# Attention with top-k and an ELU feed-forward on one core: one score burst over four PSUM banks, and a gate summed in SBUF

## The chip, the core and the metric

The kernel runs on one core of a Trainium2 chip. A core has TensorE (PE, with its weight loads shown as PEld), VectorE (DVE), ScalarE (ACT), GpSimd (POOL) and the DMA queue of SyncE (SP). The engines run their own instruction streams and wait for each other by semaphores. The metric is the time on the device in microseconds (us). PSUM, into which TensorE writes, has eight banks of 512 fp32 columns in each of 128 partitions, as the kernel's tiles use it.

## What is computed

For 8 batches of 8 heads with 576 positions of 64 features, each query keeps the 32 largest of its 576 scores; softmax over these, then the product with v. The 4608 rows of 512 features go through a feed-forward block with ELU.

```python
scores = scale * np.matmul(q, k.transpose(0, 1, 3, 2))
kth = np.partition(scores, -top_k, axis=-1)[..., -top_k:-top_k + 1]
mask = scores >= kth
scores = np.where(mask, scores, -1000000000.0)
scores = scores - np.max(scores, axis=-1, keepdims=True)
attn = np.exp(scores)
attn = attn / (np.sum(attn, axis=-1, keepdims=True) + 1e-09)
x = np.matmul(attn, v)          # heads side by side: (4608, 512)
h = x @ w_in                    # 512 -> 2048
g = np.where(h > 0.0, h, np.exp(np.minimum(h, 0.0)) - 1.0)
out = g @ w_out                 # 2048 -> 512
```

## The kernel before

The work is cut into 144 steps. A step is one tile of 128 queries for a pair of heads (`Step`). A batch has 576 = 4 x 128 + 64 query rows, so 16 normal steps and two remainder steps, in which four heads share a tile of 64-row halves (`u.heads`). Steps are ordered by batch; pairs of tiles with one pair of heads form a `Group`, which is closed (product with v) once.

A step passes through five stages, each in a later turn of the loop at L617: scores are made two steps ahead (`scores`, L280), the selection of the 32 largest runs in the current step (`select`, L322), the mask and the exponential one step later (`mask`, L345), the scaling by the reciprocal at that step's end (`normalise`, L362), the transposes of the 9 chunks of 128 score columns two steps later (`turn`, L375), and after the last tile of a group the product with v (`attend`, L397). The selection is done by VectorE alone: per row of scores four MAX8 (each finds eight maxima) and three MATCH_REPLACE8 (which take them out), for two heads.

`scores` works by halves. For each half of 288 key columns two matmuls (one a head, each in two fp32 passes) write two banks of the tile `ps`, and one ScalarE activation copies both out with the scale (L297). The pool `ps_sc` has one such tile, so the second half waits for the first's copy. Head 0 of a pair uses rows 0 to 63 of TensorE's array and head 1 rows 64 to 127: the profile prints such a matmul as 64*128 (rows by columns of the array used), a hidden matmul as 128*128 and one of `attend` as 128*64. In `attend` the chunks 0 to 3 use all 128 key rows, and the last chunk, which holds the 64 remaining keys of both heads, uses 64 rows each: 64*64.

`transpose_qk` (L236) turns k and q of a pair of heads, four transposes each, then the remaining 64 rows of both with three small transposes (64*128), which go out with one copy (L262).

The feed-forward work is cut into pieces in `ffn_pieces` (L457) and handed out by `feed` (L577), four times a step. `hidden(f)` computes 128 of the 2048 hidden features of a block of one to three tiles (L471), and ScalarE makes n = exp(-relu(-h)) with two activations (L479, L480). The gate is max(n - 1, h), one VectorE instruction with h from PSUM (L451). `close_gates` issues these late, at the next `feed`, at the next project piece, or when two are open. `project` multiplies the gates with w_out into a PSUM bank over four pieces (L489) and ScalarE copies the result out (L498). How much is handed out follows from costs (`HIDDEN`, `PROJECT`) and the step by which each block's work is due.

PSUM is used up: `ps_sc` has two banks, `ps_t` (transposes and `attend`) three, `ps_f` (hidden and project) three. From step 8 on (`tight`) the order of TensorE, ScalarE, VectorE and GpSimd is that of the program text (`manual_schedule`, L644); before, a scheduler orders it. During the first eight steps the weights, which arrive as 64-bit floats, are decoded to fp32 in pieces (`decode_piece`).

Of the kernel before, what the change touches and what calls it, by code (L numbers as in the profile page):

```python
# [9 lines left out]
ALU = mybir.AluOpType  # L10
# [70 lines left out]
def kernel(  # L81
# [35 lines left out]
    etpool = pool("et", 2)  # L117
    small = pool("small", 4)
    xtpool = pool("xt", 2)
    fpool = pool("f", 2)  # L120
    opool = pool("o", 1)
    ps_sc = pool("ps_sc", 1, space=PSUM)
    ps_t = pool("ps_t", 3, space=PSUM)
    ps_f = pool("ps_f", 3, space=PSUM)
    late = {}
    raws = ExitStack()
    early = raws.enter_context(tc.tile_pool(name="early", bufs=1))
    rawpool = raws.enter_context(tc.tile_pool(name="raw", bufs=3))

    ident = const.tile([P, P], FP32, tag="ident", name="ident")  # L130
# [59 lines left out]
    def hook():  # L190

        if not decode:
            return
        decode.pop(0)()
        if not decode:
            raws.close()
            late["g"] = ctx.enter_context(tc.tile_pool(name="g", bufs=2))
            late["x"] = ctx.enter_context(tc.tile_pool(name="x", bufs=2))

# [9 lines left out]
    loaded, kqT, vT = {}, {}, {}  # L209

    def load_qk(b, hp):
        for name, src in (("k", k), ("q", q)):
            t = ldpool.tile([P, J + 1, 2, D], FP32, tag=name + "in", name=name + "in")
            for hh in range(2):
                nc.sync.dma_start(
                    t[:, 0:J, hh, :],
                    src[b, 2 * hp + hh, 0:JP, :].rearrange("(p j) d -> p j d", j=J),
                )
            nc.sync.dma_start(
                t[0:R, J, :, :],  # L220
                src[b, 2 * hp : 2 * hp + 2, JP:S, :].rearrange("h p d -> p h d"),
            )
            loaded[b, hp, name] = t

    def load_v(b, hp):
        t = kvpool.tile([P, 2 * J + 1, D], FP32, tag="vT", name="vT")
        for hh in range(2):
            h = 2 * hp + hh
            nc.sync.dma_start(
                t[:, hh * J : (hh + 1) * J, :],  # L230
                v[b, h, 0:JP, :].rearrange("(p j) d -> p j d", j=J),
            )
            nc.sync.dma_start(t[hh * R : (hh + 1) * R, 2 * J, :], v[b, h, JP:S, :])
        vT[b, hp] = t

    def transpose_qk(b, hp):  # L236

        d = kvpool.tile([P, 4 * J + 3, D], FP32, tag="kqT", name="kqT")
        kqT[b, hp] = d[:].rearrange("p c d -> p (c d)")
        srcs = [loaded.pop((b, hp, name)) for name in ("k", "q")]
        for i, src in enumerate(srcs):
            ps = ps_t.tile([P, JP], FP32, tag="t", name="qkps")
            for c in range(J):
                nc.tensor.transpose(  # L247
                    ps[:, c * P : (c + 1) * P],
                    src[:, c, :, :].rearrange("p h d -> p (h d)"),
                    ident[:],  # L250
                )
            c0 = KEYS + i * (2 * J + 1) * D
            nc.scalar.copy(kqT[b, hp][:, c0 : c0 + JP], ps[:])
            yield
        ps = ps_t.tile([P, JP], FP32, tag="t", name="qkps")
        for i, src in enumerate((srcs[0], *srcs)):
            nc.tensor.transpose(  # L257
                ps[:, i * R : (i + 1) * R],
                src[0:R, J, :, :].rearrange("p h d -> p (h d)"),
                ident[0:R, 0:R],  # L260
            )
        nc.scalar.copy(  # L262
            d[:, 0 : 4 * J + 3 : 2 * J + 1, :],
            ps[:, 0 : 3 * R].rearrange("p (a s) -> p a s", a=3),
        )
        yield

    def start_qk(b, hp):
        turning.append(transpose_qk(b, hp))
# [7 lines left out]

    turning = []

    def scores(u, half):  # L280

        if half == 0:
            u.sc = scpool.tile([P, 2, S], FP32, tag="sc", name="sc")
        ps = ps_sc.tile([P, 2, JP], FP32, tag="s", name="scps")
        q0 = QUERIES + u.t.qt * P
        for h, i, rows in u.heads:
            kq = kqT[u.t.b, h // 2]
            part = slice(i * D, (i + 1) * D)
            k0 = (KEYS if i == 0 else 0) + half * HS
            nc.tensor.matmul(  # L290
                ps[rows, i, 0:HS],
                kq[part, q0 : q0 + u.t.ql],
                kq[part, k0 : k0 + HS],
                start=True,
                stop=True,
            )
        nc.scalar.activation(  # L297
            u.sc[:, :, half * HS : (half + 1) * HS], ps[:, :, 0:HS], AF.Copy, scale=scale
        )

    def select_row(u, i):
        if i == 0:
# [72 lines left out]
    def turn(u, chunks):  # L375

        if u.turned:
            return
        g = u.group
        if g.et is None:  # L380
            g.et = etpool.tile([P, 2 * J + 1, len(g.tiles), P], FP32, tag="et", name="et")
        ps = ps_t.tile([P, JP], FP32, tag="t", name="eps")
        sc = u.sc[:, :, :].rearrange("p i s -> p (i s)")
        n = chunks.stop - chunks.start
        for c in range(n):
            c0 = (chunks.start + c) * P
            nc.tensor.transpose(ps[:, c * P : (c + 1) * P], sc[:, c0 : c0 + P], ident[:])  # L387
        nc.scalar.copy(  # L388
            g.et[:, chunks, u.at, :],
            ps[:, 0 : n * P].rearrange("p (c q) -> p c q", c=n),  # L390
        )
        if chunks.stop == 2 * J + 1:
            u.turned = True
            if u.at == len(g.tiles) - 1:
                closing.append(g)

    def attend(g):  # L397
# [3 lines left out]
        for k in range(2 if t.rem else 1):  # L401
            hp = 2 * g.hp + k if t.rem else g.hp
            vt = vT[t.b, hp]
            for c in range(J + 1):
                for i in range(2):
                    rows = slice(0, P) if c < J else slice(i * R, (i + 1) * R)
                    chunk = J if c == J else i * (J + 1) + c
                    w = g.et[rows, chunk, :, :].rearrange("p a q -> p (a q)")
                    cols = slice(0, n)
                    if t.rem:  # L410
                        c0 = R * (k if i == 0 else 1 - k)
                        w = w[:, c0 : c0 + R]
                        cols = slice(k * R, (k + 1) * R)
                    nc.tensor.matmul(  # L414
                        ps[i * D : (i + 1) * D, cols],
                        vt[rows, 2 * J if c == J else i * J + c, :],
                        w,
                        start=(c == 0),
                        stop=(c == J),
                    )  # L420
# [23 lines left out]
            ffn.extend(ffn_pieces(blk))  # L444

    gates = []

    def close_gates():
        for dst, n, ps in gates:
            w = dst.shape[-1]  # L450
            nc.vector.scalar_tensor_tensor(  # L451
                out=dst, in0=n[:, 0:w], scalar=-1.0, in1=ps[:, 0:w],
                op0=ALU.add, op1=ALU.max,
            )
        gates.clear()

    def ffn_pieces(blk):  # L457
        n_tok = blk.slots * P

        def hidden(f):  # L460
# [3 lines left out]
            elif f % NG == 0 and blk.number > 0:  # L464
                g = late["g"].tile([P, NG, T], FP32, tag="g", name="gT")
                blk.gT.append(g[:])
            if len(gates) > 1:
                close_gates()
            ps = ps_f.tile([P, dm], FP32, tag="f", name="hps")
            for i in range(NC):  # L470
                nc.tensor.matmul(  # L471
# [3 lines left out]
                    start=(i == 0),  # L475
                    stop=(i == NC - 1),
                )
            n = fpool.tile([P, T], FP32, tag="n", name="n")
            nc.scalar.activation(n[:, 0:n_tok], ps[:, 0:n_tok], AF.Relu, scale=-1.0)  # L479
            nc.scalar.activation(n[:, 0:n_tok], n[:, 0:n_tok], AF.Exp, scale=-1.0)  # L480
            gates.append((blk.gT[f // NG][:, f % NG, 0:n_tok], n, ps))

        def project(s, part):
            close_gates()
# [91 lines left out]

    def feed(n, share):  # L577

        close_gates()
        fed["at"] = max(fed["at"], n)  # L580
        ahead = [(w - fed["sum"]) / (x - fed["at"]) for x, w in due if x > fed["at"]]
        if ahead:
            fed["over"] += max(0.0, share * min(ahead))
        fed["at"] += share
        while ffn and decoded[0] >= ffn[0][1] and 0.5 * ffn[0][0] <= fed["over"]:
            cost, _, piece = ffn.pop(0)
            fed["over"] -= cost
            fed["sum"] += cost
            piece()
# [5 lines left out]
    load_v(0, 0)  # L595
    start_qk(0, 0)
    turn_qk(True)
    scores(steps[0], 0)
    scores(steps[0], 1)
    load_qk(0, 2)  # L600
    start_qk(0, 1)
    turn_qk(True)
    scores(steps[1], 0)
    scores(steps[1], 1)
    load_qk(0, 3)
    for hp in range(1, NHP):
        load_v(0, hp)
# [9 lines left out]
    for n in range(NS + 3):  # L617
# [2 lines left out]
        ahead, cur, prev, done = step(n + 2), step(n), step(n - 1), step(n - 2)  # L620
        if n < tight:
            turn_qk(True)
            scores(ahead, 0)
            scores(ahead, 1)
            for i in range(2):
                passes = select_row(cur, i)
                next(passes)
# [17 lines left out]
            )  # L645
        passes = select(cur) if cur else iter(range(4))
        if ahead:
            scores(ahead, 0)
        next(passes)
        feed(n, 0.25)  # L650
        if prev:
            mask(prev, 0)
        turn_qk()
        while closing:
            attend(closing.pop(0))
        if ahead:
            scores(ahead, 1)
        next(passes)
        feed(n, 0.25)
        if done:  # L660
# [49 lines left out]
```

## Time and profile before

| | |
|---|---|
| Time, median of 3 runs | 1733.86 us (1732.75 to 1734.05) |
| Profiled execution, its own time | 1732.9 us |
| Span from its first to its last instruction | 1731.0 us |
| Mean granted TensorE clock | 0.975 |
| HBM traffic over the span | 31 GB/s |

The busy share by slice, 43 us each, and the clock that TensorE was granted:

```profile
PE   6468999999999999999999999999999999999999
DVE  6899999999999999999989898999999989997700
PEclk9568999999999999999999999999999999999999
```

The digits are tenths. The first four slices hold the start and the decoding of the weights, with a lower clock; the last two are feed-forward work alone. The largest groups of instructions by line:

```profile
L471 PE MATMUL hps<-xT,w_in 128*128 128x256 f32 (+2 forms) x2432 | 563.7, 378 | 22.8 <-DVE gT L451 15.6
L341 DVE MAX8 m<-wk 128x8 f32<-128x576 f32 x816 | 574.9, 745 | 0.0
L489 PE MATMUL ops<-w_out,gT 128*128 128x512 f32 x1152 | 525.3, 600 | 2.5 <-DVE gT L451 2.5
L290 PE MATMUL scps<-kqT 64*128 64x288 f32 (+1 forms) x1280 | 232.4, 462 | 32.6 <-ACT sc L297 24.3
L371 POOL TENSOR_SCALAR sc<-sc,rec 128x576 f32<-128x576 f32 x288 | 213.9, 752 | 185.1 <-DVE rec L369 175.2
L297 ACT ACTIVATE sc<-scps 128x576 f32<-128x576 f32 x288 | 185.9, 646 | 86.2 <-PE scps L290 81.4
L414 PE MATMUL avps<-et,vT 128*64 128x256 f32 (+5 forms) x2080 | 200.4, 328 | 3.8 <-ACT et L388 3.7
```

A group's line names the source line, engine, operation, output and inputs, the form and the count; behind the bar stand busy time in us, the mean of one in ns, and the engine's idle time just before such instructions with what ended most of it. Matmuls overlap, so the mean of one is longer than its share of TensorE's time; for that one compares start times.

### The profile page before, as it was taken

To read this page: it belongs to the slowest core of one execution; us is meant where nothing else is said; L and a number is where in the kernel's file an instruction comes from. 1 tells how busy PE (TensorE), PEld (TensorE's weight loads), DVE (VectorE), ACT (ScalarE), POOL (GpSimd) and SP (SyncE) were. 2 spreads that over 40 slices of the span, in tenths; PEclk is the share of its full clock that TensorE was granted. 3 is DMA by queue.
4 is the path that set the end of the run, shared out by engine and by line. 5 is a ranking of instruction groups with operands and counts; after the bars stand their busy time and mean duration, and the time that the engine had idled before them with its cause. 6 is when DMAs were issued, how large, how long until landed. Compare 5 with 4: busy or idle time off the path is not lost.

```text
span 1731.0 us, 25867 instructions
## 1 busy us (share of the span) xinstructions
PE 1647.5 (95%) x8592; PEld 1007.8 (58%) x8592; DVE 1544.7 (89%) x3392; ACT 1145.1 (66%) x2509; POOL 407.5 (24%) x1078
## 2 busy tenths in 40 slices
PE   6468999999999999999999999999999999999999
PEld 3245677557474756555456565645547475745565
DVE  6899999999999999999989898999999989997700
ACT  5786787678676867667666675757657585756521
POOL 2674222222222222221212122221222221121100
PEclk9568999999999999999999999999999999999999
DMA  6641021001100110001200111001100000000000
GB/s 155 178 135 44 15 48 34 7 7 42 48 7 7 34 46 23 1 24 31 48 12 1 41 35 34 1 13 42 42 19 1 26 15 27 7 7 7 7 13 12
DMA packets 101125, 56.19 MB, mean 32 GB/s; under 512 B 84096, under 2 KB 92288, under 8 KB 100992
## 3 DMA queue, kind: packets, MB, share of 16 engines
q1 hardware_dynamic: 100992, 54.55, 11.5%
q8 instruction: 67, 1.10, 0.3%
q14 instruction: 66, 0.54, 0.1%
HBM read 45.09 MB, written 9.44 MB: 31 GB/s over the span
## 4 chain that ended last, share of the span: by engine, by line
PE 82%; DVE 8%; ACT 2%; issue 1%; POOL 1%; DMA 0%; ACTq 0%
PE ops L489 28%; PE hps L471 27%; PE avps L414 9%; PE scps L290 9%; PE eps L387 7%; DVE wk L334 3%; DVE m L341 3%; PE qkps L247 1%; DVE m L329 1%; ACT sc L297 1%; DVE gT L451 1%; PE qkps L257 0%; ACT n L480 0%; ACT n L479 0%; DVE wk L311 0%
## 5 line engine op out<-in xcount | busy, mean ns | idle before, releaser
L471 PE MATMUL hps<-xT,w_in 128*128 128x256 f32 (+2 forms) x2432 | 563.7, 378 | 22.8 <-DVE gT L451 15.6
L341 DVE MAX8 m<-wk 128x8 f32<-128x576 f32 x816 | 574.9, 745 | 0.0
L489 PE MATMUL ops<-w_out,gT 128*128 128x512 f32 x1152 | 525.3, 600 | 2.5 <-DVE gT L451 2.5
L471 PEld LDWEIGHTS hps<-xT,w_in 128*128 128x128 f32 x2432 | 406.1, 193 | 143.1 <-DVE gT L451 26.0
L334 DVE MATCH_REPLACE8 wk<-m,wk 128x576 f32<-128x576 f32 x544 | 399.4, 741 | 0.0
L489 PEld LDWEIGHTS ops<-w_out,gT 128*128 128x128 f32 x1152 | 208.7, 190 | 240.4 <-issue 232.5
L367 POOL TENSOR_SCALAR dene<-den 128x2 f32<-128x2 f32 x144 | 33.1, 230 | 1000.2 <-ACT sc L358 999.9
L290 PE MATMUL scps<-kqT 64*128 64x288 f32 (+1 forms) x1280 | 232.4, 462 | 32.6 <-ACT sc L297 24.3
L388 ACT COPY et<-eps 128x512 f32<-128x512 f32 (+1 forms) x432 | 189.8, 474 | 102.4 <-PE eps L387 102.3
L371 POOL TENSOR_SCALAR sc<-sc,rec 128x576 f32<-128x576 f32 x288 | 213.9, 752 | 185.1 <-DVE rec L369 175.2
L357 ACT ACTIVATE sc<-sc,neg 128x576 f32<-128x576 f32 x288 | 224.0, 778 | 48.4 <-POOL neg L354 48.1
L297 ACT ACTIVATE sc<-scps 128x576 f32<-128x576 f32 x288 | 185.9, 646 | 86.2 <-PE scps L290 81.4
L358 ACT ACTIVATE sc<-sc,gap 128x576 f32<-128x576 f32 x288 | 223.1, 775 | 25.3
L479 ACT ACTIVATE n<-hps 128x256 f32<-128x256 f32 (+2 forms) x304 | 111.5, 367 | 144.9 <-PE hps L471 131.9
L387 PEld LDWEIGHTS eps<-ident,sc 128*128 128x128 f32 x1296 | 156.8, 144 | 84.6 <-issue 53.9
L414 PE MATMUL avps<-et,vT 128*64 128x256 f32 (+5 forms) x2080 | 200.4, 328 | 3.8 <-ACT et L388 3.7
L387 PE MATMUL eps<-ident,sc 128*128 128x128 f32 x1296 | 192.1, 282 | 12.3 <-POOL sc L371 11.7
L334 DVE MATCH_REPLACE8 wk<-m,sc 128x576 f32<-128x576 f32 x272 | 199.7, 741 | 0.0
L329 DVE MAX8 m<-sc 128x8 f32<-128x576 f32 x272 | 191.1, 744 | 0.0
L451 DVE SCALAR_TENSOR_TENSOR gT<-n,hps 128x256 f32<-128x256 f32 (+2 forms) x304 | 117.6, 391 | 71.4 <-ACT n L480 70.7
L414 PEld LDWEIGHTS avps<-et,vT 128*64 128x64 f32 (+1 forms) x2080 | 115.4, 138 | 95.0 <-issue 53.8
L290 PEld LDWEIGHTS scps<-kqT 64*128 64x128 f32 (+1 forms) x1280 | 91.5, 180 | 126.0 <-issue 47.9
(40 smaller groups left out, 840.8 us busy)
## 6 DMA issues: line engine op xcount, KB each, us to landing
kin<-in_k_dram SPq DMA_DIRECT2D x64, 128.0 KB, 2.8
qin<-in_q_dram SPq DMA_DIRECT2D x64, 128.0 KB, 2.9
raw<-in_moe_w_in_dram SPq DMA_DIRECT2D x16, 512.0 KB, 4.1
vT<-in_v_dram SPq DMA_DIRECT2D x64, 128.0 KB, 2.3
raw<-in_moe_w_out_dram SPq DMA_DIRECT2D x16, 512.0 KB, 3.3
out_dram<-osb SPq DMA_DIRECT2D x32, 256.0 KB, 2.2
kin<-in_k_dram SPq DMA_DIRECT2D x32, 32.0 KB, 2.5
qin<-in_q_dram SPq DMA_DIRECT2D x32, 32.0 KB, 2.5
```

Source lines behind the costliest of these rows:

```text
L290: nc.tensor.matmul(ps[rows, i, 0:HS], kq[part, q0 : q0 + u.t.ql], kq[part, k0 : k0 + HS], start=True, stop=True,)
L297: nc.scalar.activation(u.sc[:, :, half * HS : (half + 1) * HS], ps[:, :, 0:HS], AF.Copy, scale=scale)
L329: nc.vector.max(found[i], cur[i])
L334: nc.vector.match_replace(wk[i], found[i], cur[i], TAKEN)
L341: nc.vector.max(found[i], cur[i])
L357: nc.scalar.activation(sc, sc, AF.Prelu, bias=neg[:], alpha=STEEP)
L358: nc.scalar.activation(sc, sc, AF.Exp, bias=gap[:], accum_out=u.den[:, i : i + 1])
L371: nc.gpsimd.tensor_scalar(u.sc[:, i, :], u.sc[:, i, :], rec[:, i : i + 1], 1.0, ALU.mult, ALU.mult)
L387: nc.tensor.transpose(ps[:, c * P : (c + 1) * P], sc[:, c0 : c0 + P], ident[:])
L414: nc.tensor.matmul(ps[i * D : (i + 1) * D, cols], vt[rows, 2 * J if c == J else i * J + c, :], w, start=(c == 0), stop=(c == J),)
L471: nc.tensor.matmul(ps[:, 0:n_tok], w_in[:, i, f * P : (f + 1) * P], blk.xT[:, i, 0:n_tok], start=(i == 0), stop=(i == NC - 1),)
L489: nc.tensor.matmul(blk.o[:], blk.gT[f // NG][:, f % NG, s * P : (s + 1) * P], w_out[:, f, :], start=(f == 0), stop=(f == NF - 1),)
```

## The change

Five things are changed together.

1. `scores` makes both halves in one burst. One tile `wide` of four banks, made once, takes the place of `ps_sc`'s tile; each head has two banks, and ScalarE copies one head (2 x 288 columns) at a time. `ps_t` and `ps_f` go from three banks to two. In the loop from step 8 the burst stands at the step's start, followed by `attend`, which stood behind the first feed.
2. Small outputs go to the unused columns of `wide`: the transposes of the remaining k and q rows to bank 1, the single chunk of `turn` to bank 3.
3. The remaining q rows are loaded beside the remaining k rows in one tile, and two full transposes take the place of three small ones. They now come first in `transpose_qk`.
4. In v the remaining rows of the two heads get a slot each, with zeros in the other head's rows (GpSimd memsets), so that `attend` uses all 128 rows in its last chunk too.
5. The gate becomes relu(h) + (n - 1): ScalarE writes relu(h) into the gate with a third activation, and VectorE adds n - 1 there, with both inputs in SBUF. The sums are issued two feeds later, or when four are open; n gets more buffers (`earlyf` 4, `f` 5).

```diff
+    wide = ps_sc.tile([P, 4, JP], FP32, tag="s", name="scps")
-    ps_t = pool("ps_t", 3, space=PSUM)
-    ps_f = pool("ps_f", 3, space=PSUM)
+    ps_t = pool("ps_t", 2, space=PSUM)
+    ps_f = pool("ps_f", 2, space=PSUM)
...
     def load_v(b, hp):
-        t = kvpool.tile([P, 2 * J + 1, D], FP32, tag="vT", name="vT")
+        t = kvpool.tile([P, 2 * J + 2, D], FP32, tag="vT", name="vT")
...
-            nc.sync.dma_start(t[hh * R : (hh + 1) * R, 2 * J, :], v[b, h, JP:S, :])
+            mine = slice(hh * R, (hh + 1) * R)
+            other = slice((1 - hh) * R, (2 - hh) * R)
+            nc.gpsimd.memset(t[other, 2 * J + hh, :], 0.0)
+            nc.sync.dma_start(t[mine, 2 * J + hh, :], v[b, h, JP:S, :])
...
     def transpose_qk(b, hp):
+        ps = wide[:, 1, HS : HS + 3 * R]
+        for i in range(2):
+            nc.tensor.transpose(
+                ps[:, i * R : i * R + P],
+                srcs[0][:, J, :, :].rearrange("p h d -> p (h d)"),
+                ident[:],
+            )
...
-    def scores(u, half):
+    def scores(u):
+        u.sc = scpool.tile([P, 2, S], FP32, tag="sc", name="sc")
         q0 = QUERIES + u.t.qt * P
+        for half in range(2):
+            for h, i, rows in u.heads:
...
+                nc.tensor.matmul(
+                    wide[rows, 2 * i + half, 0:HS],
...
+        for i in range(2):
+            nc.scalar.activation(
+                u.sc[:, i, :].rearrange("p (a s) -> p a s", a=2),
+                wide[:, 2 * i : 2 * i + 2, 0:HS], AF.Copy, scale=scale,
             )
...
+        if chunks.stop - chunks.start == 1:
+            ps = wide[:, 3, HS : HS + P]
+        else:
+            ps = ps_t.tile([P, JP], FP32, tag="t", name="eps")
...
-                    rows = slice(0, P) if c < J else slice(i * R, (i + 1) * R)
-                    w = g.et[rows, chunk, :, :].rearrange("p a q -> p (a q)")
+                    w = g.et[:, chunk, :, :].rearrange("p a q -> p (a q)")
...
-                        vt[rows, 2 * J if c == J else i * J + c, :],
+                        vt[:, 2 * J + i if c == J else i * J + c, :],
...
+    place = [0]
+    def close_gates(keep=0):
+        while gates and gates[0][0] <= place[0] - keep:
+            _, dst, n = gates.pop(0)
             nc.vector.scalar_tensor_tensor(
-                out=dst, in0=n[:, 0:w], scalar=-1.0, in1=ps[:, 0:w],
-                op0=ALU.add, op1=ALU.max,
+                out=dst, in0=n, scalar=-1.0, in1=dst, op0=ALU.add, op1=ALU.add
             )
...
-            if len(gates) > 1:
-                close_gates()
+            if len(gates) > 3:
+                gates[0] = (-1, *gates[0][1:])
+                close_gates(place[0])
...
-            nc.scalar.activation(n[:, 0:n_tok], ps[:, 0:n_tok], AF.Relu, scale=-1.0)
-            nc.scalar.activation(n[:, 0:n_tok], n[:, 0:n_tok], AF.Exp, scale=-1.0)
+            nc.scalar.activation(n, ps[:, 0:n_tok], AF.Relu, scale=-1.0)
+            nc.scalar.activation(g, ps[:, 0:n_tok], AF.Relu)
+            nc.scalar.activation(n, n, AF.Exp, scale=-1.0)
...
     def feed(n, share):
-        close_gates()
+        place[0] += 1
+        close_gates(2)
...
         if ahead:
-            scores(ahead, 0)
+            scores(ahead)
+        while closing:
+            attend(closing.pop(0))
         next(passes)
         feed(n, 0.25)
         if prev:
             mask(prev, 0)
         turn_qk()
-        while closing:
-            attend(closing.pop(0))
-        if ahead:
-            scores(ahead, 1)
         next(passes)
```

## The prediction

> **What bounds the kernel now.** I read the page's busy rows and slices first, then the chain, then windows, then TensorE's timeline inside a step.
>
> ```profile
> PE 1647.5 (95%) x8592; PEld 1007.8 (58%) x8592; DVE 1544.7 (89%) x3392; ACT 1145.1 (66%) x2509; POOL 407.5 (24%) x1078
> PE 82%; DVE 8%; ACT 2%; issue 1%; POOL 1%; DMA 0%; ACTq 0%
> ...
> 147.00:600.00 453.00, 439.82 (x2672) 286.87 (x2671) 449.18 (x1018) 324.69 (x752) 104.13 (x306) 1.00 0.09 24
> 600.00:800.00 200.00, 197.86 (x1062) 119.13 (x1060) 194.63 (x428) 136.76 (x296) 44.64 (x133) 1.00 0.09 25
> 800.00:1640.00 840.00, 834.58 (x4124) 491.56 (x4124) 772.45 (x1686) 553.88 (x1184) 173.97 (x519) 1.00 0.08 21
> 1640.00:1731.00 91.00, 87.07 (x308) 51.24 (x306) 6.90 (x17) 20.10 (x47) 1.70 (x3) 0.99 0.03 12
> ```
>
> Each window row gives its length, then busy time of PE, PEld, DVE, ACT, POOL. There are four regimes. Up to 147 us the weights are decoded. From 147 to 600 DVE has 449 of 453 us: DVE sets the pace. From 800 to 1640 DVE rests 68 us and PE shows no gap: PE sets it. After 1640 only TensorE's last FFN work is left. A busy PE hides its own losses, though; the starts show them:
>
> ```profile
> 898.55 1.99 PE L471 MATMUL hps<-xT,w_in 128*128 128x256 f32 x8
> 900.48 0.76 PE L290 MATMUL scps<-kqT 64*128 64x288 f32 x4
> 901.16 1.99 PE L471 MATMUL hps<-xT,w_in 128*128 128x256 f32 x8
> 902.99 0.71 PE L387 MATMUL eps<-ident,sc 128*128 128x128 f32 x5
> 903.54 1.89 PE L471 MATMUL hps<-xT,w_in 128*128 128x256 f32 x8
> 905.27 0.60 PE L387 MATMUL eps<-ident,sc 128*128 128x128 f32 x4
> ...
> 908.21 1.99 PE L471 MATMUL hps<-xT,w_in 128*128 128x256 f32 x8
> 910.13 2.53 PE L414 MATMUL avps<-et,vT 128*64 128x256 f32 x20
> 912.59 0.76 PE L290 MATMUL scps<-kqT 64*128 64x288 f32 x4
> 913.28 1.99 PE L471 MATMUL hps<-xT,w_in 128*128 128x256 f32 x8
> ```
>
> A full-array hidden group takes 905.27-903.54 = 1.73 us, 0.216 a pass. After a score burst it takes 902.99-901.16 = 1.83; between two bursts 900.48-898.55 = 1.93. The burst itself takes 0.68, while its four passes of 288 columns, two at a time, need 2 x 0.243 = 0.49. So one burst of array shape 64*128 costs 0.19 + 0.10 before + 0.10 behind = 0.40 us beyond its work: two changes of shape at 0.20. The attend group takes 2.46 where ten pairs of passes need 2.16: 0.15 of the 0.30 is its inner change from 128*64 to 64*64 (the first form ends with 16 passes, the last 4 are 64*64), the rest its edges.
>
> [...]
>
> ```profile
> L179 DVE SCALAR_TENSOR_TENSOR raw<-raw x32: 665/674/1741, 11.0 to 151.4; 128x512 uint32<-128x512 uint32 x32
> ...
> L451 DVE SCALAR_TENSOR_TENSOR gT<-n,hps 128x256 f32<-128x256 f32 (+2 forms) x304 | 117.6, 391 | 71.4 <-ACT n L480 70.7
> ...
> DVE rec L369 <- POOL dene L367: 45.2, 29, 3.9
> ...
> PEld hps L471 <- DVE gT L451: 26.0, 29, 2.9
> ```
>
> [...] the gate's sum, with one PSUM input, starts at 901.96 and the next instruction at 902.28, 0.32 us for 256 columns[...]; L179's starts are 0.59 us apart for 512[...]. The measurement decides: the operand's move frees no DVE time.
>
> **The change part by part.** Score burst: one per step in place of two, so one pair of shape changes goes: 0.40 us. In a step with an attend the order was hidden, burst, work, attend, its 64*64 part, burst, work: six changes, 0.40 + 0.15 + 0.15 + 0.20 + 0.20 = 1.10. It becomes hidden, burst, attend, work, with the remainder chunk on full zero-filled rows: 0.20 + 0.15 + 0.20 = 0.55 us. The padded rows cost nothing, since a pass costs its columns. A remainder group has two further inner changes, about 0.33 us with them. From the code the loop from step 8 has 134 steps with scores, 64 plain attends and 16 of remainders: 54 x 0.40 + 64 x 0.55 + 16 x 0.88 = 71 us of TensorE, 0.52 a step. Transposes of the remainders: three of 64 columns in 64*128 become two of 128 in full shape; in most cases the old ones stood directly before a burst of the same shape, so I take 0 of it (between -3 and +3 us).
>
> ACT: 304 further Relus out of PSUM; the 256-column form of L479 has 377 ns, so about 110 us, 66% to 72% busy. ACT is covered: between 147 and 1640 us it waits for PE 117 us on hps, 86 on eps, 74 on scps. It delays the mask behind it by 0.3 us a hidden, which I take as nothing in the DVE-bound part and inside the joint loss below in the PE-bound part; without cover it is 0.6 us a step. Hidden banks go from three to two, but a bank is free after the second Relu, about 0.7 us behind its last pass, and no longer after exp and DVE's sum of the next feed; a following hidden takes 1.73. The 26 us in which weight loads waited for gT may go: 0 to 26, I take none. The transposes lose a bank and give their small parts to the corners of the burst's banks; these are copied out half a step before the next burst, so 0. One burst means ACT can't start the first eviction after 0.68 us, but the scores are for two steps ahead: 0.
>
> POOL: 64 memsets, unmeasured in this shape; the row for 128x128 at the start took 0.20 us, so at most 13 us of an engine with 76% idle; the buffer they wait for was freed a step before. The DMAs keep their number; SP issues them as before.
>
> DVE: the sum's two inputs now both lie in SBUF. Per sum I bound this at [...] +0.38 (half of one 0.75 us scaling on POOL, L371). POOL is busy 22% in the loop; 0.22 x 0.38 = 0.08 for random meetings, but the sums of the fourth feed start ahead of the scaling. I take 0.05, so 0.1 us a step at two sums. The later closing (two feeds back) ends the waits of DVE for the exponential, 24 us in this stretch; part of that was only PE's lateness.
>
> The sum, by step (a step runs from its first MAX8 of L329 to that of the next). DVE needs 9.7 us for the selection (its shortest steps, which have no gate) plus the sums; PE's need I added up from starts, waits left out. Steps 8 to 53: DVE needs 10.3 and steps take 10.5; PE's 0.52 is not seen, +0.1 for the sums, less some coupling: +1 us in all. Steps 54 to 71: PE 10.44, DVE 10.34, taken 10.73, so 0.29 is lost by each waiting for the other in turn. After: PE 9.92, DVE 10.44, loss 0.19: -2. Steps 72 to 140: PE 10.94, DVE 10.33, taken 11.16. After: PE 10.42, DVE 10.43, and the loss of 0.29 that the like-balanced steps show: 10.72, so -0.44 x 69 = -30. Last steps and tail, which keep few shape changes: -3. First 147 us: four banks end the wait of the second burst for the first's eviction, but the first transposes now wait for the last of six loads: -1, between -6 and +6. Together -35: 1732.9 (span 1731.0 and 1.9 around it) becomes 1698. The median shown, 1733.86, is 1 us above the profiled execution; I leave the forecast at 1698.
>
> **Rivals.** (B) DVE and PE are coupled more loosely, since sums are two feeds late and banks free early: the joint loss goes. For: those waits are in the rows above. Late 91 steps keep 0.52 each, 47, and some 10 us of gate waits: 1676. (C) ACT or the lock eats most: 0.2 us a step left in the late steps, -18, and +5 early: 1720. For: DVE's wait for POOL dene, 45 us, is really a wait for ACT's mask, and ACT gets work ahead of it. (D) Slower: the gate sums are shut out by the scaling on POOL. At x a sum, DVE grows by 2x in every step: early 46 steps lose 92x at once, the late ones have 0.44 to give. It breaks even near x = 0.15; at 0.25 the early part loses 23, the middle 7, the late part gains 3 and the ends 4: 1756. For: L179's longest, 1741. Against: its median, with POOL 59 to 72% busy between 40 and 160 us by the windows. (E) Nothing visible: gains and lock cancel, 1733.
>
> **How the numbers follow.** Forecast, with 1684 to 1712 about it, 0.50; B 0.17; C 0.17; E 0.03; D 0.13. A difference of 0.2%, 3.5 us, is about what can be told from no change. Faster is forecast, B and C: 0.84; same 0.03; slower 0.13. The range 1676 to 1728 leaves out D, E and the low edge of B.
>
> **What would show it.** One run of eight L290 passes per step taking about 1.17 us to the next start; avps all 128*64, 2.31 or so; no 64*64 there. Hidden groups of 1.83 once a step. In steps 72 to 140, 10.7 us a step and DVE near 97% busy; in 8 to 53 unchanged within 0.2. The sum's median near 400 ns for 256 columns, with few over 600; ACT near 72%. The forecast is wrong if sums often exceed 600 ns, if hidden passes begin to wait for the Relus, or if the first 150 us shift by over 6.

## The result, and the profile after

The changed kernel takes 1713.6 us (median of 4 runs, 1713.55 to 1714.49) against 1733.5 us for the kernel before beside it. The ratio is 0.9887, 95% interval 0.9869 to 0.9904. That is 1.1% faster and inside the stated range of 1676 to 1728, but only 20 of the forecast 35 us came: the time lies 1.6 us outside the band of 1684 to 1712 that the forecast itself had, on the side of rival C. The profiled execution has a span of 1711.8 us, 19.2 below that of before.

The same two rows of the page, busy time and chain, read now:

```profile
PE 1593.9 (93%) x8560; PEld 1029.6 (60%) x8560; DVE 1551.1 (91%) x3392; ACT 1180.3 (69%) x2813; POOL 432.7 (25%) x1142
...
PE 64%; DVE 23%; ACT 8%; issue 3%; POOL 1%; DMA 1%; SPq 0%; ACTq 0%; POOLq 0%
```

TensorE has 54 us less busy time, yet the span fell by 19: most of what was saved became idle time. In the chain of work that ended last, TensorE's share of the span falls from 82% to 64%, VectorE's rises from 8% to 23% and ScalarE's from 2% to 8%. The forecast had no growth of ScalarE's share.

To compare kernels of different length, windows at fixed times mislead, since they hold different work. The windows below go by step: steps 8 to 53 and 72 to 140, first of before, then of after. Each row gives its length, then busy time of PE, PEld, DVE, ACT and POOL, clock, DMA share and GB/s.

```profile
147.00:628.00 481.00, 466.84 (x2830) 305.28 (x2829) 476.65 (x1079) 345.48 (x800) 108.86 (x321) 1.00 0.10 26
...
821.00:1598.00 777.00, 772.57 (x3879) 457.13 (x3878) 719.57 (x1574) 513.96 (x1102) 162.20 (x483) 1.00 0.08 21
```

```profile
144.00:632.00 488.00, 458.23 (x2836) 314.41 (x2838) 482.38 (x1089) 358.10 (x923) 118.81 (x339) 1.00 0.10 25
...
822.00:1579.00 757.00, 747.57 (x3881) 470.10 (x3880) 719.25 (x1574) 530.90 (x1227) 174.03 (x513) 1.00 0.08 21
```

In the late steps (second rows) VectorE does the same 1574 instructions in the same 719 us; its share rises from 92.6% to 95.0% because the stretch is shorter. TensorE, which showed 4 us of gaps before, shows 9. It no longer sets the pace alone, but VectorE, with 38 us beside its instructions where 719 us of work stand, does not yet set it either.

TensorE's timeline in these steps (start, duration, then the run of passes):

```profile
899.84 1.24 PE L298 MATMUL scps<-kqT 64*128 64x288 f32 x8
901.01 3.72 PE L484 MATMUL hps<-xT,w_in 128*128 128x256 f32 x16
904.57 0.60 PE L400 MATMUL eps<-ident,sc 128*128 128x128 f32 x4
905.01 0.27 PE L400 MATMUL scps<-ident,sc 128*128 128x128 f32 x1
905.12 1.89 PE L484 MATMUL hps<-xT,w_in 128*128 128x256 f32 x8
...
909.11 1.24 PE L298 MATMUL scps<-kqT 64*128 64x288 f32 x8
910.28 2.38 PE L426 MATMUL avps<-et,vT 128*64 128x256 f32 x20
912.59 2.64 PE L484 MATMUL hps<-xT,w_in 128*128 128x256 f32 x11
```

The burst of eight takes 901.01 - 899.84 = 1.17 us, the attend group 912.59 - 910.28 = 2.31 us in one shape: both as forecast to the hundredth. So the change does on TensorE what it says. Where time is lost now shows in the waits of after (each row: engine, line, what it waited for: us in all over the whole span, times, longest):

```profile
DVE rec L379 <- POOL dene L377: 58.4, 33, 14.3
...
PE hps L484 <- ACT gT L497: 16.9, 21, 1.9
...
PE scps L400 <- ACT kqT L261: 13.5, 14, 2.2
...
PE scps L256 <- ACT sc L306: 11.9, 9, 1.9
```

The first two have counterparts in before, where VectorE waited 61.9 us for `dene` and TensorE 15.6 us for the gate's sum ahead of a hidden group. The last two are new: the small transposes that now write into corners of the burst's tile wait for ScalarE. The pair L400 <- L261 is odd. L400's single chunk goes to bank 3, while L261 reads k's and q's small parts out of bank 1. They share no byte and no bank; they share the tile `wide`. This is one such case, with both queues:

```profile
815.09 0.60 PE L400 MATMUL eps<-ident,sc 128*128 128x128 f32 x4
...
815.80 0.78 ACT L367 ACTIVATE sc<-sc,neg 128x576 f32<-128x576 f32 x1
...
816.67 0.78 ACT L368 ACTIVATE sc<-sc,gap 128x576 f32<-128x576 f32 x1
...
817.45 0.30 ACT L261 COPY kqT<-scps 128x192 f32<-128x192 f32 x1
...
817.89 0.45 PE L400 MATMUL scps<-ident,sc 128*128 128x128 f32 x1 [2.20 <-ACT kqT L261]
```

The small transposes of k and q had run at 814.43. Their copy stands on ScalarE behind the three gate activations and two passes of the mask, so it runs at 817.45, and TensorE stands still for 2.20 us before a transpose of 0.1.

### The profile page after: what moved, and what is told of

The parts are those of the page before. It is cut to its first block, busy times and chain, and to the rows that moved or that the text cites. A ratio compares the mean times of both kernels' runs of the same rounds, so it can differ in the third digit from the quotient of the medians.

```text
span 1711.8 us, 26507 instructions
## 1 busy us (share of the span) xinstructions
PE 1593.9 (93%) x8560; PEld 1029.6 (60%) x8560; DVE 1551.1 (91%) x3392; ACT 1180.3 (69%) x2813; POOL 432.7 (25%) x1142
## 4 chain that ended last, share of the span: by engine, by line
PE 64%; DVE 23%; ACT 8%; issue 3%; POOL 1%; DMA 1%; SPq 0%; ACTq 0%; POOLq 0%
PE ops L507 25%; PE hps L484 19%; DVE wk L344 8%; PE avps L426 7%; DVE m L351 7%; PE scps L298 6%; PE eps L400 4%; DVE m L339 2%; DVE gT L465 2%; ACT sc L367 2%; ACT sc L368 2%; DVE wk L321 1%; DVE m L327 1%; ACT et L401 1%; ACT n L498 1%
## 5 line engine op out<-in xcount | busy, mean ns | idle before, releaser
L484 PE MATMUL hps<-xT,w_in 128*128 128x256 f32 (+2 forms) x2432 | 555.7, 377 | 24.8 <-ACT gT L497 16.9
L368 ACT ACTIVATE sc<-sc,gap 128x576 f32<-128x576 f32 x288 | 223.2, 775 | 26.3 <-ACT sc L367 1.5
L306 ACT ACTIVATE sc<-scps 128x576 f32<-128x576 f32 x288 | 173.0, 660 | 80.5 <-PE scps L298 80.4
L401 ACT COPY et<-eps 128x512 f32<-128x512 f32 x288 | 167.2, 581 | 74.3 <-PE eps L400 74.2
L426 PE MATMUL avps<-et,vT 128*64 128x256 f32 (+2 forms) x2080 | 190.4, 324 | 14.3 <-ACT et L401 13.7
L400 PE MATMUL eps<-ident,sc 128*128 128x128 f32 x1152 | 177.8, 280 | 24.7 <-POOL sc L381 24.6
L400 PEld LDWEIGHTS eps<-ident,sc 128*128 128x128 f32 x1152 | 145.2, 145 | 92.2 <-issue 48.4
L298 PE MATMUL scps<-kqT 64*128 64x288 f32 (+1 forms) x1280 | 186.5, 440 | 11.1 <-ACT et L401 6.1
L465 DVE SCALAR_TENSOR_TENSOR gT<-n,gT 128x256 f32<-128x256 f32 (+2 forms) x304 | 128.9, 430 | 49.6 <-ACT n L498 49.6
L426 PEld LDWEIGHTS avps<-et,vT 128*64 128x64 f32 x2080 | 120.6, 140 | 87.8 <-issue 28.7
L298 PEld LDWEIGHTS scps<-kqT 64*128 64x128 f32 (+1 forms) x1280 | 100.2, 182 | 76.6 <-issue 22.2
```

The source lines that it names most:

```text
L298: nc.tensor.matmul(wide[rows, 2 * i + half, 0:HS], kq[part, q0 : q0 + u.t.ql], kq[part, k0 : k0 + HS], start=True, stop=True,)
L368: nc.scalar.activation(sc, sc, AF.Exp, bias=gap[:], accum_out=u.den[:, i : i + 1])
L401: nc.scalar.copy(g.et[:, chunks, u.at, :], ps[:, 0 : n * P].rearrange("p (c q) -> p c q", c=n),)
L426: nc.tensor.matmul(ps[i * D : (i + 1) * D, cols], vt[:, 2 * J + i if c == J else i * J + c, :], w, start=(c == 0), stop=(c == J),)
L484: nc.tensor.matmul(ps[:, 0:n_tok], w_in[:, i, f * P : (f + 1) * P], blk.xT[:, i, 0:n_tok], start=(i == 0), stop=(i == NC - 1),)
```

## The experiments

The kernel before, run beside each of them, had medians from 1732.9 to 1734.3 us. The working theory after the result had two parts: the shared tile adds waits between users of different banks, and ScalarE with its third activation is not covered. The rival was balance: VectorE simply has no more to give, and the 15 us were never there.

**1. The four-bank tile as two tiles of two banks, one a head.** Nothing else changes.

```diff
-    wide = ps_sc.tile([P, 4, JP], FP32, tag="s", name="scps")
+    wide = [ps_sc.tile([P, 2, JP], FP32, tag=f"s{i}", name=f"scps{i}") for i in range(2)]
...
-        ps = wide[:, 1, HS : HS + 3 * R]
+        ps = wide[0][:, 1, HS : HS + 3 * R]
...
-            ps = wide[:, 3, HS : HS + P]
+            ps = wide[1][:, 1, HS : HS + P]
```

> The changed kernel, with the four-bank tile made as two tiles of two banks, one a head, and nothing else changed. Shared-tile theory (small transposes in the corner wait for ScalarE's last read anywhere in the one tile, not only of their own bank): the waits of the corner transposes of the chunk (some 18 us between 144 and 1619 us) vanish and those of k and q shrink, time 1699 to 1706 us. Balance theory (what is lost of the forecast comes from steps whose feed-forward share makes TensorE late while VectorE is full in others): these waits are covered, 1710 to 1716 us.

Measured: 1695.83 us (1695.16 to 1697.53), ratio to before 0.9785, 95% interval 0.9769 to 0.9802; 17.8 us below after, and 3 us below the range that the shared-tile theory gave. It is faster than both kernels. The wait of L400 for L261 is absent from its waits, that of L256 for the eviction falls from 11.9 to 7.8 us, all waits of TensorE in steps 8 to 140 together fall from 46 to 31 us, and the window of steps 72 to 140 reads:

```profile
819.00:1562.00 743.00, 740.48 (x3861) 466.26 (x3858) 718.25 (x1574) 528.69 (x1224) 174.09 (x514) 1.00 0.08 22
```

The same work of VectorE now fills 96.7% of the late stretch, and TensorE's gaps are back to 2.5 us. On TensorE in the same step, some 3 us earlier in this kernel, the small transpose follows without delay:

```profile
811.65 0.60 PE L400 MATMUL eps<-ident,sc 128*128 128x128 f32 x4
812.09 0.27 PE L400 MATMUL scps<-ident,sc 128*128 128x128 f32 x1
```

The theory of the shared tile stands and the theory of balance falls. The edit also separates one head's burst from the other head's eviction, but ScalarE waits 80.4 us for the burst ahead of its evictions in both kernels, so that was not the gain. This kernel is called "split" below.

**2. After with the old gate** (maximum with the PSUM bank, two activations, closed at the next feed or when two are open), so that the two hidden banks meet the old holder.

```diff
-                out=dst, in0=n, scalar=-1.0, in1=dst, op0=ALU.add, op1=ALU.add
+                out=dst, in0=n[:, 0:w], scalar=-1.0, in1=ps[:, 0:w],
+                op0=ALU.add, op1=ALU.max,
...
-            nc.scalar.activation(g, ps[:, 0:n_tok], AF.Relu)
...
-        close_gates(2)
+        close_gates()
```

> The changed kernel with the gate as it was before (max from PSUM on VectorE at the next feed, two activations, no Relu into the gate), with two hidden banks. ScalarE theory (the third activation delays the masks and with them VectorE's reciprocal): faster than the changed kernel, 1700 to 1708 us. Bank theory (the new gate is what makes two hidden banks enough): slower, 1725 to 1745 us, with hidden passes waiting for VectorE's sum. Balance theory alone: within 4 us of 1713.6.

Measured: 1748.34 us (1745.84 to 1750.72), ratio 1.0087 (1.0072 to 1.0102): 35 us above after and 15 above before. A row of its waits says why:

```profile
PE hps L485 <- DVE gT L465: 60.5, 63, 3.8
```

With two banks and VectorE as the last reader of a bank, TensorE stops 63 times for the sum. Freeing the bank after the second Relu is what makes two hidden banks enough, and so pays for the four-bank burst.

**3. Before with the new gate alone** (three hidden banks kept; three activations, late sum in SBUF, as in the change).

> The kernel before with the new gate alone (third activation, sum in SBUF two feeds later), three hidden banks, bursts and attend as before. ScalarE theory: slower than before by 8 us or more. Lock theory (sums in SBUF are shut out by GpSimd): slower by 3 to 10 us, with sums far above 400 ns. Looser coupling: faster by 3 to 10 us. The bursts' share of the gain is then what is left of the 20 us.

Measured: 1738.3 us (1734.91 to 1740.88, 7 runs), ratio 1.003 (1.0019 to 1.0041). Step 8 starts at 150.8 us instead of 146.9; the steps 8 to 140 take 1452.3 us against 1451.6. In the order of before the new gate neither gains nor costs in the loop. By the total alone this fits the lock theory (3 to 10 us slower), but the sums have a median of 406 ns, not far above 400, and the 5 us lie ahead of the loop and behind it. Neither half of the change is worth anything alone.

**4 to 6. What the third activation costs.** In 4 the Relu into the gate is issued twice in after. In 5 it is left out of after, in 6 out of split; the sum then adds n - 1 and n, so relu(h) is missing from the gate.

```diff
             nc.scalar.activation(g, ps[:, 0:n_tok], AF.Relu)
+            nc.scalar.activation(g, ps[:, 0:n_tok], AF.Relu)
```

```diff
-                out=dst, in0=n, scalar=-1.0, in1=dst, op0=ALU.add, op1=ALU.add
+                out=dst, in0=n, scalar=-1.0, in1=n, op0=ALU.add, op1=ALU.add
...
-            nc.scalar.activation(g, ps[:, 0:n_tok], AF.Relu)
```

> The changed kernel with the Relu into the gate issued twice (304 further activations of the same kind, the output is unchanged). ScalarE theory: slower by 8 us or more, as the first of them cost as much. Balance or shared-tile theory: ScalarE has cover, within 4 us of 1713.6.

> The changed kernel without the third activation: relu(h) is left out and VectorE adds n - 1 and n, so the output is another; the sum keeps two SBUF inputs and its place. ScalarE theory, with e4's slope (61 us for 304 activations more): 1680 to 1695 us. If the slope of e4 is that of an engine pushed over its edge and the third activation still had cover: 1706 to 1714 us.

> The version with the four banks as two tiles (e1, 1695.8 us), also without the third activation; relu(h) is left out. If the lateness of ScalarE and the waits of the shared tile are separate costs: as much below e1 as e5 is below the changed kernel, 1670 to 1685 us. If both were one (late ScalarE is what made the shared tile's waits long): at most 6 us below e1.

Measured: 4: 1774.37 us (1771.64 to 1776.64), ratio 1.0237 (1.0222 to 1.0252), 61 above after. 5: 1705.06 us (1704.72 to 1706.18), ratio 0.9836 (0.982 to 0.9853), 8.6 below after. 6: 1689.62 us (1689.33 to 1689.75), ratio 0.9745 (0.9731 to 0.976), 6.2 below split. Waits of kernel 4:

```profile
DVE rec L379 <- POOL dene L377: 108.5, 61, 13.8
...
PE hps L484 <- ACT gT L498: 32.6, 40, 2.0
```

Each is about twice its size in after (58.4 and 16.9). `dene` on GpSimd waits for the mask's second activation (L368, 138 times in after), so the first line is VectorE waiting for ScalarE. ScalarE is 73% busy in this kernel and is still what decides. The cost is not straight: the third activation costs 6 to 9 us, a fourth 61. ScalarE's starts show why. These are the activations of one hidden group of 256 columns in before, in after and in kernel 4:

```profile
903.48 0.37 ACT L479 ACTIVATE n<-hps 128x256 f32<-128x256 f32 x1
903.88 0.42 ACT L480 ACTIVATE n<-n 128x256 f32<-128x256 f32 x1
```

```profile
908.78 0.37 ACT L496 ACTIVATE n<-hps 128x256 f32<-128x256 f32 x1
909.04 0.38 ACT L497 ACTIVATE gT<-hps 128x256 f32<-128x256 f32 x1
909.31 0.42 ACT L498 ACTIVATE n<-n 128x256 f32<-128x256 f32 x1
```

```profile
1110.31 0.36 ACT L496 ACTIVATE n<-hps 128x256 f32<-128x256 f32 x1
1110.58 0.37 ACT L497 ACTIVATE gT<-hps 128x256 f32<-128x256 f32 x1
1110.98 0.38 ACT L498 ACTIVATE gT<-hps 128x256 f32<-128x256 f32 x1
1111.26 0.41 ACT L499 ACTIVATE n<-n 128x256 f32<-128x256 f32 x1
```

From the first of these starts to the start of what stands behind the group, the medians at 256 columns are 738 ns with two activations, 836 with three and 1278 with four. With two, the exponential starts 415 ns behind the Relu whose result it reads, while activations that need nothing of each other start some 270 ns apart. So the third one goes for the most part into a pause that ScalarE had anyway and costs its queue 0.10 us. The fourth writes the same tile as the third, starts 415 ns behind it and brings a pause of its own: 0.44 us. Kernel 4 is therefore not the third activation taken twice. ScalarE's busy time says the same: 1145.1 us in before, 1180.3 in after, 1287.8 in 4.

Kernel 5 came 1 us below its second branch (1706 to 1714). For 6 I read the slope of 4 backwards and missed by 5 to 20 us. Its other branch, at most 6 below split if both losses are one, fits by number (6.2); yet the loss to the shared tile and the loss to the activation nearly add, 17.8 and 8.6 apart, 24.0 together (1713.6 - 1689.6), so they are separate in the main. Without the third activation the PSUM bank is also free one activation sooner; what of the 6 to 9 us is due to that was not separated.

**7. After with 64 rows in the last chunk of v again,** which restores the inner change of array shape in every attend.

```diff
-                    w = g.et[:, chunk, :, :].rearrange("p a q -> p (a q)")
+                    rows = slice(0, P) if c < J else slice(i * R, (i + 1) * R)
+                    w = g.et[rows, chunk, :, :].rearrange("p a q -> p (a q)")
```

> The changed kernel with the last chunk of attend on 64 rows again (64*64), so one change of array shape more in each attend and three in one of remainders. My price of 0.15 us each: 64 x 0.15 + 16 x 0.48 = 17 us more of TensorE; about half of it seen, 1718 to 1728 us. If TensorE's changes of shape are covered: within 3 us of 1713.6.

Measured: 1726.61 us (1724.79 to 1729.62), ratio 0.9961 (0.9946 to 0.9976): 13.0 above after. The changes of shape that the trace shows in steps 8 to 140 rise from 345 to 456. The time beyond the passes' own (216 ns for 256 full-array columns) at those with no wait ahead of them, read from start to start, rises from 54 to 71 us: 17 us for 111, about 0.15 each.

**8. Split with the burst cut in two,** the second half behind the first feed, both evicted after it.

```diff
         if ahead:
-            scores(ahead)
+            scores(ahead, (0,))
...
         feed(n, 0.25)
+        if ahead:
+            scores(ahead, (1,))
```

> e1 (1695.8 us) with the score burst in two again: the first half at the step's start, the second behind the first feed, both copied out by head after the second. My price of 0.40 us a step: 134 x 0.40 = 54 us more of TensorE, of which the DVE-bound steps (8 to 53) show little and the later ones nearly all: 1720 to 1740 us. If the changes of shape are not what the burst saves: within 6 us of e1.

Measured: 1797.05 us (1796.36 to 1797.49), ratio 1.0365 (1.035 to 1.038): 101 above split, a miss. In steps 8 to 140 TensorE's time beyond the passes' own, waits set apart, grows by about 49 us, near the priced 134 x 0.40 = 54. Its waits grow by another 50 us, and I had not thought of them:

```profile
DVE rec L380 <- POOL dene L378: 136.9, 77, 14.3
...
PE scps L401 <- ACT sc L307: 28.6, 35, 1.3
PE scps L256 <- ACT sc L307: 25.3, 28, 1.4
```

The evictions now start after the second half, and the single chunk in the corner of head 1 comes right behind it, so it waits for them. The run therefore comes near the price but isn't a clean test of it: it moves the corners' waits too.

**9. Split with the sum on GpSimd** in two instructions, n - 1 and the addition.

```diff
-            nc.vector.scalar_tensor_tensor(
-                out=dst, in0=n, scalar=-1.0, in1=dst, op0=ALU.add, op1=ALU.add
-            )
+            nc.gpsimd.tensor_scalar(n, n, -1.0, 0.0, ALU.add, ALU.add)
+            nc.gpsimd.tensor_tensor(dst, dst, n, ALU.add)
```

> e1 (1695.8 us) with the gate's sum on GpSimd in two instructions (n - 1, then the add), in place of VectorE's one. Balance theory: VectorE loses its 0.1 to 1.1 us of sums a step, every step needs 9.7 us of it, TensorE alone is left as a bound: the steps to 53 fall by some 0.4 us each, 1670 to 1688 us. GpSimd-queue theory (its sums stand ahead of the small instructions that the mask and the scaling wait for, in order): the gain is given back, 1695 to 1730 us.

Measured: 1725.8 us (1724.96 to 1726.56), ratio 0.9952 (0.9937 to 0.9967): 30 above split. VectorE is relieved and waits instead:

```profile
DVE rec L379 <- POOL dene L377: 156.9, 95, 13.1
...
ACT sc L367 <- POOL neg L364: 84.3, 50, 7.0
```

The short GpSimd instruction `neg`, which feeds the mask, queues behind the long sums: 144 of its 288 runs start right behind one. `dene` does so only 4 times of 144; it is late because the mask is.

**10. Split with the small transposes of k and q last again,** as before the change.

> e1 with the small transposes of k and q last again, as in the kernel before. Their wait for the scores' eviction (8 us where they follow the burst directly) goes: 1688 to 1694 us. If that wait is covered by VectorE's steps: within 3 us of e1's 1695.8.

Measured: 1749.32 us (1745.0 to 1755.93), ratio 1.0091 (1.0067 to 1.0115): 53 above split, a clear miss. One place of its timeline shows what I had overlooked:

```profile
813.52 0.38 PE L267 MATMUL scps<-ident,kin 128*128 128x128 f32 x2
815.87 0.35 ACT L272 COPY kqT<-scps 128x192 f32<-128x192 f32 x1
...
816.26 2.29 PE L299 MATMUL scps<-kqT 64*128 64x288 f32 x8 [2.36 <-ACT kqT L272]
```

Put last, the corner is written just ahead of the next burst, and the burst waits for the copy out of it, 31 times and 50.2 us in all by the view of the waits. "Half a step before the next burst" is true only of the changed order.

**11 and 12. Two activations again, in another way.** exp(h) is taken at once, and min(exp(h), 1) - 1 replaces exp(-relu(-h)) - 1. In 11 (from 9) GpSimd does the minimum and the sum; in 12 (from split) GpSimd does the minimum one feed later and VectorE the sum two feeds later. The minimum is shown as in 12.

```diff
+                nc.gpsimd.tensor_scalar(e[2], e[2], 1.0, -1.0, ALU.min, ALU.add)
...
-            nc.scalar.activation(n, ps[:, 0:n_tok], AF.Relu, scale=-1.0)
             nc.scalar.activation(g, ps[:, 0:n_tok], AF.Relu)
-            nc.scalar.activation(n, n, AF.Exp, scale=-1.0)
+            nc.scalar.activation(n, ps[:, 0:n_tok], AF.Exp)
```

> e9 with two activations: n = exp(h) from PSUM, GpSimd makes min(n, 1) - 1 of it (the same gate), relu(h) as before. ScalarE theory, by e5 and e6 (6 to 9 us for one activation): 6 to 9 us below e9. If GpSimd's queue is what bounds e9: within 3 us of e9.

> e1 (1695.8 us) with two activations a hidden group: n = exp(h) from PSUM and relu(h); GpSimd makes min(n, 1) - 1 one feed later, VectorE adds it into the gate two feeds later, so the gate is the same function. ScalarE theory (e6 is 6 us below e1 with one activation less): 1686 to 1693 us. GpSimd-queue theory (e9 and e11 put two instructions a gate there and lost): one instruction a gate costs half of e11's excess, 1695 to 1702 us.

Measured: 11: 1703.72 us (1700.99 to 1703.85), ratio 0.9825 (0.9809 to 0.9842), 22 below 9, where 6 to 9 were expected, and 8 above split. Its two activations need nothing of each other: at 256 columns what follows starts 527 ns behind the first, against 834 in 9. These 0.31 us fit the larger gain, though no run isolates it. 12: 1765.4 us (1764.1 to 1766.57), ratio 1.0185 (1.0171 to 1.0199), 70 above split, a miss of every theory. Waits of 12:

```profile
ACT sc L367 <- POOL neg L364: 216.3, 101, 5.1
...
POOL n L464 <- ACT n L504: 132.9, 94, 23.3
```

GpSimd works in the order of the program text. Its minimum waits 94 times for an exponential that ScalarE has not reached; right behind it stand 126 of the 288 `neg`, for which the mask on ScalarE waits 101 times. By these waits the lateness goes round in a ring. Of the versions that compute the reference, split is the fastest.

## Why the prediction was right, and where it was off

The steps of the sum, with what after and split measured (differences to before in us, by step starts in the traces; they add up to the differences of the spans):

| term | forecast | after | split |
|---|---|---|---|
| first 147 us | -1 | -2.9 | -0.2 |
| steps 8 to 53 | +1 | +6.6 | +2.0 |
| steps 54 to 71 | -2 | -2.8 | -4.3 |
| steps 72 to 140 | -30 | -20.2 | -33.9 |
| last steps and tail | -3 | 0.0 | 0.0 |
| sum | -35 | -19.3 | -36.3 |

**The step that failed.** "The transposes lose a bank and give their small parts to the corners of the burst's banks; these are copied out half a step before the next burst, so 0." The question asked there was only whether the burst waits for the corners. It hardly does in after (0.6 us for L261). The other directions were left out: a corner's transpose waits for the eviction of the burst, and, since all four banks are one tile, for the copy out of any other corner. That was 17.8 us (split against after), a little more than the 15.6 that lie between 1713.6 and the forecast; it hits the early steps (6.6 instead of 2.0) as well as the late ones.

**The mis-sized terms.** The third activation "is covered", which I took as nothing in the DVE-bound part; it costs 8.6 us in after and 6.2 in split. The total of ACT's waits said nothing about its latency: the mask, the evictions and the copies for which others wait stand in the same queue. ScalarE's own time for it was priced too high: of the "about 110 us" 35 came (busy time 1145.1 to 1180.3 us), and a group of 256 columns delays what stands behind it by about 0.10 us and not by 0.3, because I priced the activation by its duration and not by starts. TensorE's saving was "71 us"; steps 8 to 140 of before show 687 changes of shape, those of after 345, and the time beyond the passes' own at the changes with no wait ahead of them falls from 107 to 54 us. That is 53 rather than 71: 342 changes at about 0.16, where I had priced 0.15 to 0.20 and an order with more of them.

The tail's -3 did not come. The base was misread as well: 777.0 us in 69 steps are 11.26 a step, not 11.16, so 10.72 would have been -37 us and not -30. Against the smaller saving, the loss of TensorE and VectorE waiting in turn, "0.29" a step, was probably taken too high: with 53 / 134 = 0.40 a step saved, TensorE would need 10.94 - 0.40 = 10.54, and split's late steps take 743.2 / 69 = 10.77, which leaves 0.23 (an estimate, as it takes the saving to be even over the steps); without the third activation they take 10.74. So the forecast 10.72 a step was met within 0.05 by errors that cancel in part, which is luck; and only a kernel without the corner waits shows it. One of the prediction's own signs of being wrong, hidden passes that wait for the Relus, came in small: 16.9 us.

**What held.** The shape of the loop: early steps gain nothing because VectorE has no time to give (476.65 of 481 us busy in before), late ones gain until both engines are level. The prices of the burst and of the attend group, to 0.01 us. A change of array shape costs TensorE time, as 7 and 8 show: about 0.15 us a change inside an attend and about 0.37 (49 us / 134) for a second burst with its changes and the slower pass behind it. The padded rows cost nothing: in after's attends of 256 columns the last chunk's pairs of passes start 0.22 us apart, as those of the other chunks do. The move of the sum's operand from PSUM to SBUF frees no VectorE time: starts of successive instructions lie 323 ns apart at 256 columns, before 320. The memsets took 146 ns at the median. Two hidden banks suffice with the new gate and not with the old (16.9 us of TensorE's waits in after, 60.5 in experiment 2).

**The rivals.** D, the sums shut out by GpSimd, rested on one long row of before (L179, 1741 ns) and on an estimate of mine, and did not come: the source view of the sum in after gives count, minimum, median and maximum in ns, then the first and last start (the counts by form are of every second one).

```profile
L465 DVE SCALAR_TENSOR_TENSOR gT<-n,gT x304: 265/404/1278, 104.7 to 1681.4; 128x256 f32<-128x256 f32 x88, 128x128 f32<-128x128 f32 x40, 128x384 f32<-128x384 f32 x24
```

Between 147 us and the end the durations beyond the plain ones add up to 6.2 us, below the 0.05 a sum that I took as an estimate (about 13 us). Long ones occur, but they are few here: 24 of 291 lasted over 60 ns more than the median of their width, and each of these began while an instruction on GpSimd was running. The longest of 256 columns (684 ns at 577.34 us) began while a scaling on GpSimd was running and ended 271 ns after that scaling; in before, with one input from PSUM, no sum took over 556 ns. B, looser coupling, is partly true, as the loss in turn was smaller. C came nearest in time (1720) and in kind for its first half: ScalarE does eat part of the gain, early and late. It did not name the corners, which took more.

**What stays open.** The fourth activation delays ScalarE's queue four to five times as much as the third (0.44 us against 0.10 a group) but costs seven times as much; which instruction's delay makes the rest was not separated, since most waits for ScalarE grow together in 4. The start of step 8 moves between 143.5 and 150.8 us among these kernels, 3 by 3.9 us later than before; the order of work in that first stretch changes with each edit, and no run isolates it.

## What to carry to other kernels

When a small result is put into unused columns of a large tile, it inherits every wait of that tile, in both directions and from all its banks (17.8 us here, split against after); price the wait of each user for each other, and declare the tile as finely as its users are independent. An engine with 30% idle time is covered only if nobody waits for the items in its queue (with ScalarE 69% busy the third activation cost 8.6 us in after): read what stands behind the added instruction and who waits for that, and take its cost from starts: one that needs nothing of its neighbours can fill a pause (0.10 us here for an activation of 0.37), one that must wait for them brings a pause along (0.44 us in 4), so a doubled instruction is no measure of the first. A change can consist of halves of which neither gains alone (2 and 3 took 15 and 5 us more than before); undo each half before judging it.

## What was not expected of the hardware

GpSimd's instruction with two operations and two constants took over 1 us for 256 columns. The source view of the minimum in kernel 12:

```profile
L464 POOL TENSOR_SCALAR n<-n x304: 630/1071/1760, 100.6 to 1733.2; 128x256 f32<-128x256 f32 x88, 128x128 f32<-128x128 f32 x40, 128x384 f32<-128x384 f32 x24
```

The median over all widths is 1071 ns, in 9 with two additions 1079 and in 11 1076. By width it is 648, 1072 and 1507 ns at 128, 256 and 384 columns in 12, some 3.4 ns a column, while the scaling of 576 columns by one number per partition, also two operations on the same engine, has a median of 745 ns there, 1.3 a column. Minimum or addition made no difference; whether the constants, the additions or something beside them do was not separated. In 9 the second instruction of a gate takes another 727 ns, so a gate keeps GpSimd for about 1.8 us, and `neg` stands behind it.
